# Attention with decay and an MLP on one core: one early load of q and k, one later product of v, one PSUM pair taken from another pool

## The chip, the core and the metric

The kernel runs on one core of one Trainium2 chip. The metric is the device time of one execution in microseconds (us). The core's engines that matter here are TensorE (PE; its weight loads are listed as PEld), VectorE (DVE), ScalarE (ACT), GpSimd (POOL) and SyncE (SP), which here only issues transfers. Each engine works through its own instructions in order; they meet through semaphores. Transfers between device memory (DRAM) and SBUF, the on-chip memory, run on 16 DMA engines and are issued from SP's or POOL's queue. Matrix products are written to PSUM, which is cut into banks; this kernel mostly takes banks in pairs.

## The reference

Eight batches, eight heads, 576 positions, head dimension 64. In each head: causal attention whose scores carry a decay taken from the running sum of log f. The heads are then put side by side (512 columns) and go through an MLP of width 2048 with a tanh gelu.

```python
scores = scale * np.matmul(q, k.transpose(0, 1, 3, 2))
log_f = np.log(np.clip(f, 0.0001, 1.0))
cum = np.cumsum(log_f, axis=-1)
scores = np.where(causal, -1000000000.0, scores + cum[:, :, :, None] - cum[:, :, None, :])
attn = softmax(scores)
x = np.matmul(attn, v)            # then heads side by side: (4608, 512)
h = x @ w_in
out = gelu_tanh(h) @ w_out        # (4608, 512), float32
```

## The kernel before

Four heads of a batch are a **quad**; a batch has two, so there are 16 quads (0 to 15), and batch b holds quads 2b and 2b + 1. Buffers of a quad come in twos and are taken by the quad's number modulo 2: `k_c` and `q_c` (as loaded), `kT` and `qT` (transposed), `pt` (the exps of the scores), `vw` (v times a weight per position). `v_nat` and `xT` are taken by the batch's number modulo 2.

**Decay.** The factor exp(cum) of the query cancels against the denominator, so only exp(-cum) of the key is needed. It is worked out once in the startup (`wT`, and `w_bf` in bfloat16) and multiplied into v: `make_vw` (L137) does so for one quad with two products, 128 by 1280 and 64 by 256 elements.

**Attention of a quad i.** `load_qk(i)` (L97) issues two transfers on POOL's queue, k and then q. `transpose_qk(i)` (L128) transposes both on VectorE. `score_round(i, r)` (L155) is one of three rounds: 16 or 24 score products into two pairs of PSUM banks from the pool "s", which holds two pairs, and then two exps on ScalarE that move them into `pt` (L190). `mask(i, r)` (L196) sets the part of a strip beyond the diagonal to zero on POOL; round 0 has two such instructions, round 1 one, round 2 two. `denominators(i)` (L251) multiplies `pt` with the weights into the pair "po" (this pool holds one pair) and makes reciprocals on VectorE (a transpose `den` that reads "po", a reciprocal, a transpose `rb`). The product goes through the strips in order, and its last two parts need the two masks of round 2. `attn_out(i, y)` (L254) makes one half of the output in "po", and `normalise` (L248) multiplies it on VectorE with the reciprocals into `xT`.

**MLP of a batch.** `mlp_in(b, fts)` (L276) makes tiles of the 2048 features, eight products each, in a pair from "s" (`ps_h`), with a gelu on ScalarE behind each (L272). `mlp_out` (L287) makes tiles of 128 output rows, 16 steps of products each (`pso`, a pool of two banks); after the sixteenth VectorE copies the tile to `o_st` and SP stores it. `mlp_out` is a generator: `pull(fill, n, 32)` runs n of its steps, each as four products of 32 rows, to fill TensorE's time between pieces of attention.

**Steps.** `step(i, j, fill, fills)` (L401) interleaves the scores of quad i with the output of quad j in three rounds. In each: the scores of (i, r), then `denominators(j)` in round 0 or `attn_out(j, r - 1)` in rounds 1 and 2, then masks, then some steps of the fill. Around the change the order is: startup (quads 0 and 1 and the first two feature tiles of batch 0), `transpose_qk(2)`, the other 14 feature tiles of batch 0, three steps of the fill, `step(2, None)`, `step(3, 2)`, `step(4, 3)`, and then the MLP of batch 1. In the startup, q and k of quads 2 and 3 and half of v of batch 1 are issued on POOL's queue behind the weights of the MLP; the other half of v of batch 1 is issued on SP's queue behind q of quad 3 (L365). The order of instructions on each engine is written out by hand, as the program text has it (`tc.manual_schedule`).

Lines that the change and the prediction speak of: L105 loads of v, L99 loads of k and q, L123 loads of w_out, L130 transposes, L140 vw, L162 scores, L190 exps, L202 masks, L218 products of attention, L240 to L244 reciprocals, L249 normalise, L263 and L272 feature tiles and gelus, L295 to L301 output tiles, copies and stores.

Of the kernel before, what the change touches and what calls it, by code (L numbers as in the profile page):

```python
# [16 lines left out]
def kernel(  # L17
# [79 lines left out]
    def load_qk(i):  # L97
        b, h0 = i // QPB, 4 * (i % QPB)
        return [nc.gpsimd.dma_start(  # L99
            out=dst[i % 2].rearrange("p a d -> p (a d)"),  # L100
            in_=src[b, h0:h0 + 4].rearrange("h (p a) d -> (h p) (a d)", p=32))
            for src, dst in ((k, k_c), (q, q_c))]

    def load_v(b, eng=nc.sync, heads=slice(0, H)):
        return [eng.dma_start(  # L105
            out=v_nat[b % 2][r:, t, heads, :],
            in_=v[b, heads, s0:s0 + 128 - r, :].rearrange("h p d -> p h d"),
        ) for t, r, s0 in [(t, 0, 128 * t) for t in range(TAIL)] + [(TAIL, 128 - LAST, S - LAST)]]
# [19 lines left out]
    def transpose_qk(i):  # L128
        for src, dst in ((k_c, kT), (q_c, qT)):
            nc.vector.transpose(  # L130
                out=dst[i % 2].rearrange("p s c -> p (s c)").bitcast(FP32)
                    .rearrange("p (t a) -> p a t", a=S // 32),
                in_=src[i % 2].rearrange("p a d -> p (a d)").bitcast(FP32)
                    .rearrange("p (a d) -> p a d", d=D // 2),
            )

    def make_vw(i, eng=nc.gpsimd):  # L137
        h0 = 4 * (i % QPB)
        for p, n, slot in ((128, NT, 0), (64, 1, HEAD)):
            eng.tensor_mul(  # L140
                vw[i % 2][:p, slot:slot + n], v_nat[(i // QPB) % 2][:p, 0:n, h0:h0 + 4, :],
                wT[:p, i, 0:n, :].unsqueeze(3).to_broadcast([p, n, 4, D]))

    def bank_pair(tag, name):
        return pools[tag].tile([128, 2, 512], FP32, name=name, tag=tag)
# [9 lines left out]
    def score_round(i, r, tags=("s", "s"), masked=False):  # L155
        off, parts = rounds[r]
        n = sum(x[2] for x in parts)
        tiles = [bank_pair(x, "ps_s") for x in tags]
        kk, qq, p = kT[i % 2], qT[i % 2], pt[i % 2]
        def block(c, m0, m, k0, q0, nq, c0, fresh):  # L160
            for h in range(4):
                nc.tensor.matmul(  # L162
                    tiles[h // 2][m0:m0 + m, h % 2, c0:c0 + nq],
                    kk[32 * h:32 * h + 32, k0:k0 + m, c],
                    qq[32 * h:32 * h + 32, q0:q0 + nq, c],
                    start=(c == 0 and fresh), stop=(c == 1),
                    skip_group_check=True,
                )

        if r == 0:  # L170
            for c in range(2):
                block(c, 0, 64, 0, 0, 512, 0, True)
                block(c, 64, 64, 64, 64, 448, 64, True)
                block(c, 64, 64, S - LAST, S - LAST, LAST, 0, False)
        else:
            c0 = 0
            for (t, q0, nq) in parts:
                for c in range(2):
                    block(c, 0, 128, 128 * t, q0, nq, c0, c0 == 0)
                c0 += nq  # L180
        if masked:
            for g in range(2):
                c0 = 0
                for (t, q0, nq) in parts:
                    for x in range(2 if q0 == 128 * t else 0):
                        nc.tensor.matmul(tiles[g][:, x, c0:c0 + 128], ident, lows[t > 0],
                                         start=False, stop=True, skip_group_check=True)
                    c0 += nq
        for g in range(2):
            nc.scalar.activation(p[:, 2 * g:2 * g + 2, off:off + n],  # L190
                                 tiles[g][:, :, 0:n], AF.Exp, scale=scale)
# [4 lines left out]
    def mask(i, r):  # L196
        p = pt[i % 2]
        for (t, q0, nq) in rounds[r][1]:
            if q0 == 128 * t:
                o = strip_off[t]  # L200
                for p0, p1, pattern in (diag if t else diag_first):
                    nc.gpsimd.affine_select(  # L202
                        out=p[p0:p1, :, o:o + 128], in_=p[p0:p1, :, o:o + 128],
                        compare_op=ALU.is_ge, fill=0.0, base=0, pattern=[[0, 4]] + pattern,
                        channel_multiplier=-1)
# [45 lines left out]
    def denominators(i):  # L251
        reciprocals(i, product(i, den_groups(i), bank_pair("po", "po")))

    def attn_out(i, y, tag="po"):  # L254
        normalise(i, y, product(i, out_groups(i, y), bank_pair(tag, "po")))

    def mlp_mm(b, ft, ph, dts):
        hS = S // 2
        n = 256 * (ft // 2) % (D_FF // 2)
        w = w_in_sb[2 * ft // N_FT][:, :, n + ft % 2:n + 256:2]  # L260
        for dt in dts:
            for j in range(2):
                nc.tensor.matmul(  # L263
                    ph[:, j, 0:hS],
                    w[:, dt],
                    xT[b % 2][:, dt, hS * j:hS * (j + 1)],
                    start=(dt == 0), stop=(dt == N_DT - 1),
                )

    def gelu(b, ft, ph):  # L270
        hS, o = S // 2, S * (b % 2)
        nc.scalar.activation(  # L272
            gT[:, ft, o:o + S].rearrange("p (j n) -> p j n", j=2),
            ph[:, :, 0:hS], AF.Gelu_apprx_tanh)

    def mlp_in(b, fts):  # L276
        tiles = [bank_pair("s", "ps_h") for _ in fts]
        for dts in (range(N_DT - 1), range(N_DT - 1, N_DT)):
            for ft, ph in zip(fts, tiles):
                mlp_mm(b, ft, ph, dts)  # L280
        for ft, ph in zip(fts, tiles):
            gelu(b, ft, ph)
# [21 lines left out]
    def out_tiles(b):  # L304
        n0 = 9 * (b // 2)

        return range(n0, n0 + 4) if b % 2 == 0 else range(n0 + 4, n0 + 9)
# [93 lines left out]
    def step(i, j, fill, fills):  # L401
        for r in range(3):
            if i is not None:
                score_round(i, r)
            if j is not None:
                if r == 0:
                    denominators(j)
                else:
                    attn_out(j, r - 1, "s" if i is None and r == 1 else "po")
            if (i, r) in ((2, 0), (3, 1)):  # L410
                transpose_qk(i + 1)
            if i is not None and r > 0:
                mask(i, r - 1)
            if i is not None and r == (2 if i == 2 else 0):
                make_vw(i, nc.vector if i < 4 else nc.gpsimd)
            pull(fill, fills[r], 32)
            if i is not None and r == 2:
                mask(i, 2)
                if i < 5:
                    load_qk(i + 2)  # L420
                if i == 2:
                    load_v(2)

    def prepare(*quads):

        for i in quads:
            if i < NQ:
                transpose_qk(i)
                if i + 2 < NQ:
                    load_qk(i + 2)  # L430

    with tc.manual_schedule():
        with tc.tile_pool(name="psX", bufs=1, space=bass.MemoryType.PSUM) as pools["x"]:
            startup()
        pools["m"] = ctx.enter_context(
            tc.tile_pool(name="psM", bufs=2, space=bass.MemoryType.PSUM))
        fill = none
        for b in range(B):

            if b == 0:  # L440
                transpose_qk(2)
            else:
                mlp_in(b, (0, 1))
                for x in fill:
                    pass
                prepare(2 * b + 3, 2 * b + 4)
                if b + 2 < B:
                    load_v(b + 2)
            for ft in range(2, N_FT):
                mlp_in(b, (ft,))  # L450
            fill = mlp_out(out_tiles(b))
            if b == 0:
                pull(fill, 3)
                step(2, None, fill, (14, 8, 8))
                step(3, 2, fill, (5, 6, 5))
                step(4, 3, fill, (4, 4, 3))
            elif b + 1 < B:
                i = 2 * b + 3
                fills = (((13, 11, 13), (12, 11, 13)) if b % 2 else ((11, 8, 10), (9, 8, 10)))
                pull(fill, 2)  # L460
                step(i, i - 1, fill, fills[0])
                step(i + 1 if i + 1 < NQ else None, i, fill, fills[1])
        for x in fill:
            pass
# [30 lines left out]
```

## Time and profile before

| | us |
|---|---|
| runs before, median of 3 | 348.53 |
| lowest, highest | 347.43, 350.45 |
| profiled execution | 348.43 |
| its span | 346.7 |
| busy in the span: PE | 334.6 (97%) |
| PEld | 198.6 (57%) |
| ACT | 198.8 (57%) |
| DVE | 126.0 (36%) |
| POOL | 114.5 (33%) |

The profile is one execution. Times in a timeline count from the span's start. A row of a timeline merges like instructions that follow one another: start, length, engine, line, operation, what it writes and reads, how many, and in brackets how long the engine had been idle before it and what ended that wait. A busy TensorE isn't TensorE at its peak, since products are pipelined and their ends are modelled. The chain of waits follows the work that ended last backwards; here each piece is given with its start and length. The row of the clock (PEclk) gives in tenths what share of TensorE's full speed was granted in each of 40 equal slices of the span.

### The profile page before, as it was taken

Reading aid. Unit: us, or ns where it says so; the run is one execution under the profiler, and the core shown is the slowest. Engines: PE = TensorE matmul, PEld = TensorE weight load, DVE = VectorE, ACT = ScalarE, POOL = GpSimd, SP = SyncE. Lnnn points to the kernel's source line nnn. Section 1 sums busy time; section 2 is a strip of 40 time slices with the busy share of each in tenths; the row PEclk is TensorE's granted clock in tenths of the full one; section 3 lists DMA queues with packets and bytes.
Section 4 is the critical chain, followed back from the end, with each engine's and each line's share of the span. In section 5 each row is a group of like instructions: output and inputs, shape, how many; then the busy total and the mean of one; then the engine's idle time right before and its main releaser. Section 6 shows DMA issues by size and latency. Waiting matters only on the chain.

```text
span 346.7 us, 11040 instructions
## 1 busy us (share of the span) xinstructions
PE 334.6 (97%) x5032; PEld 198.6 (57%) x5050; DVE 126.0 (36%) x169; ACT 198.8 (57%) x244; POOL 114.5 (33%) x157
## 2 busy tenths in 40 slices
PE   7999998899999999999999999999999999999995
PEld 2457744377445774467554674457644675557642
DVE  7592066551342504433234413325133312430021
ACT  4866676476645567566655567566754566516400
POOL 6642246634262232615143241624035400200000
PEclk9999999899999999999999999999999999999999
DMA  7799979659211590019311391118201100110021
GB/s 131 171 173 211 210 186 212 130 93 229 53 64 62 115 190 34 32 62 205 72 62 35 105 203 29 40 57 179 59 32 65 48 15 2 35 62 30 2 84 68
DMA packets 45439, 33.37 MB, mean 96 GB/s; under 512 B 34288, under 2 KB 34288, under 8 KB 45392
## 3 DMA queue, kind: packets, MB, share of 16 engines
q0 software_dynamic: 7232, 14.81, 23.9%
q1 hardware_dynamic: 38160, 17.85, 19.0%
q8 instruction: 39, 0.64, 0.8%
q14 instruction: 8, 0.07, 0.1%
HBM read 36.85 MB, written 9.44 MB: 133 GB/s over the span
## 4 chain that ended last, share of the span: by engine, by line
PE 83%; DMA 5%; issue 3%; ACT 3%; DVE 3%; POOL 2%; POOLq 0%; ACTq 0%; DVEq 0%
PE ps_h L263 36%; PE pso L295 31%; PE po L218 8%; PE ps_s L162 7%; DMA q_c<-in_q_dram 4%; ACT pt L190 3%; DMA v_nat<-in_v_dram 1%; POOL v_nat L105 1%; POOL pt L202 1%; DVE xT L249 1%; DVE vw L140 1%; DVE rb L244 0%; POOL k_c L99 0%; DVE den L240 0%; DVE qT L130 0%
## 5 line engine op out<-in xcount | busy, mean ns | idle before, releaser
L295 PE MATMUL pso<-w_out_sb,gT 128*32 128x512 bf16 (+1 forms) x1892 | 132.4, 381 | 0.7
L263 PE MATMUL ps_h<-xT,w_in_sb 128*128 128x288 bf16 x1024 | 128.5, 286 | 1.1 <-DVE xT L249 0.6
L190 ACT ACTIVATE pt<-ps_s 128x1024 bf16<-128x1024 f32 x96 | 93.0, 1021 | 52.7 <-PE ps_s L162 50.1
L272 ACT ACTIVATE gT<-ps_h 128x576 bf16<-128x576 f32 x128 | 82.5, 651 | 65.2 <-PE ps_h L263 65.2
L263 PEld LDWEIGHTS <-w_in_sb 128*128 128x128 bf16 x1024 | 99.5, 98 | 31.0 <-issue 4.9
L295 PEld LDWEIGHTS <-gT 128*32 128x32 bf16 (+1 forms) x1908 | 59.3, 97 | 53.7 <-issue 1.3
L202 POOL TENSOR_SCALAR_AFFINE_SELECT pt<-pt 128x512 bf16<-128x512 bf16 (+1 forms) x70 | 46.3, 670 | 132.5 <-ACT pt L190 131.6
L300 DVE COPY o_st<-pso 128x512 f32<-128x512 f32 x36 | 24.6, 685 | 63.4 <-PE pso L295 63.2
L240 DVE STREAM_TRANSPOSE den<-po 128x576 f32<-128x576 f32 x16 | 12.5, 782 | 81.9 <-PE po L218 81.9
L249 DVE TENSOR_TENSOR xT<-po,rb 128x576 bf16<-128x576 f32 x32 | 24.0, 756 | 45.4 <-PE po L218 45.2
L162 PE MATMUL ps_s<-qT,kT 32*64 32x64 bf16 (+6 forms) x896 | 36.5, 295 | 4.1 <-DVE qT L130 3.1
L140 POOL TENSOR_TENSOR vw<-v_nat,wT 128x1280 bf16<-128x1280 f32 (+1 forms) x24 | 34.8, 1472 | 1.9 <-DVE o_st L300 1.8
L162 PEld LDWEIGHTS <-kT 32*128 32x128 bf16 (+1 forms) x896 | 15.2, 98 | 30.0 <-issue 24.0
L218 PE MATMUL po<-pt,vw 128*32 128x64 bf16 (+4 forms) x768 | 27.5, 280 | 0.5 <-DVE xT L249 0.3
L130 DVE STREAM_TRANSPOSE kT<-k_c 128x576 f32<-128x576 f32 x16 | 20.0, 1247 | 16.8 <-DMA k_c<-in_k_dram 16.8
L218 PEld LDWEIGHTS <-vw 128*32 128x32 bf16 x768 | 13.4, 97 | 14.7 <-issue 8.2
L130 DVE STREAM_TRANSPOSE qT<-q_c 128x576 f32<-128x576 f32 x16 | 19.9, 1244 | 2.8 <-DMA q_c<-in_q_dram 2.7
L99 POOL DMA_DIRECT2D k_c<-in_k_dram x16 | 9.1, 567 | 29.6 <-DVE kT L130 26.6
L218 PE MATMUL po<-pt,w_bf 128*32 128x512 bf16 (+5 forms) x384 | 14.1, 280 | 0.0
L244 DVE STREAM_TRANSPOSE rb<-rec 128x576 f32<-128x576 f32 x16 | 12.4, 778 | 0.5
L190 ACT ACT_TABLE_LOAD x7 | 9.0, 1283 | 5.9 <-PE ps_s L162 5.9
L99 POOL DMA_DIRECT2D q_c<-in_q_dram x16 | 8.6, 537 | 7.2 <-DVE qT L130 5.2
(38 smaller groups left out, 72.7 us busy)
## 6 DMA issues: line engine op xcount, KB each, us to landing
out_dram<-o_st SPq DMA_DIRECT2D x36, 256.0 KB, 2.0
v_nat<-in_v_dram SPq DMA_DIRECT2D x24, 256.0 KB, 8.1
k_c<-in_k_dram POOLq DMA_DIRECT2D x16, 288.0 KB, 6.1
q_c<-in_q_dram POOLq DMA_DIRECT2D x16, 288.0 KB, 7.3
w_in_sb<-in_moe_w_in_dram POOLq DMA_DIRECT2D x4, 512.0 KB, 9.9
w_out_sb<-in_moe_w_out_dram POOLq DMA_DIRECT2D x4, 512.0 KB, 17.6
v_nat<-in_v_dram SPq DMA_DIRECT2D x14, 128.0 KB, 4.3
v_nat<-in_v_dram POOLq DMA_DIRECT2D x8, 128.0 KB, 7.2
```

What stands on the lines that cost most here:

```text
L99: return [nc.gpsimd.dma_start(out=dst[i % 2].rearrange("p a d -> p (a d)"), in_=src[b, h0:h0 + 4].rearrange("h (p a) d -> (h p) (a d)", p=32))
L130: nc.vector.transpose(out=dst[i % 2].rearrange("p s c -> p (s c)").bitcast(FP32) .rearrange("p (t a) -> p a t", a=S // 32), in_=src[i % 2] ...
L140: eng.tensor_mul(vw[i % 2][:p, slot:slot + n], v_nat[(i // QPB) % 2][:p, 0:n, h0:h0 + 4, :], wT[:p, i, 0:n, :].unsqueeze(3).to_broadcast([ ...
L162: nc.tensor.matmul(tiles[h // 2][m0:m0 + m, h % 2, c0:c0 + nq], kk[32 * h:32 * h + 32, k0:k0 + m, c], qq[32 * h:32 * h + 32, q0:q0 + nq, c ...
L190: nc.scalar.activation(p[:, 2 * g:2 * g + 2, off:off + n], tiles[g][:, :, 0:n], AF.Exp, scale=scale)
L202: nc.gpsimd.affine_select(out=p[p0:p1, :, o:o + 128], in_=p[p0:p1, :, o:o + 128], compare_op=ALU.is_ge, fill=0.0, base=0, pattern=[[0, 4]] ...
L218: nc.tensor.matmul(po[r0:r0 + w.shape[-1], o:o + nq], w, p[:, h, col:col + nq], start=(n < 2), stop=(n in (0, len(product_parts) - 1)), sk ...
L249: nc.vector.tensor_mul(xT[i // QPB % 2][:, 2 * (i % QPB) + y, :], po, rbs[i])
L263: nc.tensor.matmul(ph[:, j, 0:hS], w[:, dt], xT[b % 2][:, dt, hS * j:hS * (j + 1)], start=(dt == 0), stop=(dt == N_DT - 1),)
L272: nc.scalar.activation(gT[:, ft, o:o + S].rearrange("p (j n) -> p j n", j=2), ph[:, :, 0:hS], AF.Gelu_apprx_tanh)
L295: nc.tensor.matmul(ps[m:m + w, :], gT[:, ft, c + m:c + m + w], w_out_sb[:, ft, :], start=(ft == 0), stop=(ft == N_FT - 1), skip_group_chec ...
L300: nc.vector.tensor_copy(st, ps)
```

## The change

Three edits.

1. In front of the feature tiles of batch 0, `transpose_qk(2)` becomes `prepare(2)`: the same two transposes, and then `load_qk(4)`. In return, step 2 doesn't issue `load_qk(4)` at its end any more, only `load_v(2)`. On POOL's queue the two loads thus move from behind the five masks of step 2 to in front of them, right behind the loads of v of the startup. Steps 3 and 4 issue the loads of quads 5 and 6 as before.
2. `make_vw(3)` moves from the first round of step 3 to its third. On VectorE its two products now stand behind the second `normalise` of quad 2, and no more behind its reciprocals.
3. The third feature tile of batch 0 (`ft == 2`) takes its pair of banks from "po", not from "s".

The order of instructions on TensorE, ScalarE and SP stays the same; VectorE has the two products, and POOL the two loads, in another place.

```diff
-    def mlp_in(b, fts):
-        tiles = [bank_pair("s", "ps_h") for _ in fts]
+    def mlp_in(b, fts, tag="s"):
+        tiles = [bank_pair(tag, "ps_h") for _ in fts]
...
-            if i is not None and r == (2 if i == 2 else 0):
+            if i is not None and r == (2 if i < 4 else 0):
                 make_vw(i, nc.vector if i < 4 else nc.gpsimd)
             pull(fill, fills[r], 32)
             if i is not None and r == 2:
                 mask(i, 2)
-                if i < 5:
-                    load_qk(i + 2)
                 if i == 2:
                     load_v(2)
+                elif i < 5:
+                    load_qk(i + 2)
...
             if b == 0:
-                transpose_qk(2)
+                prepare(2)
...
-                mlp_in(b, (ft,))
+                mlp_in(b, (ft,), "po" if b == 0 and ft == 2 else "s")
```

`prepare` is there already and is not changed:

```python
def prepare(*quads):
    for i in quads:
        if i < NQ:
            transpose_qk(i)
            if i + 2 < NQ:
                load_qk(i + 2)
```

## The prediction

> **What bounds the kernel now.** I read the page first: the span and the clock row (40 slices of 8.67 us).
>
> ```profile
> span 346.7 us, 11040 instructions
> ...
> PEclk9999999899999999999999999999999999999999
> ```
>
> The profiled execution took 348.43 us, 1.73 us more than its span and 0.10 us under the median of the runs (348.53 us), so I work on 348.43 and change nothing outside the span. One slice, the eighth (60.7 to 69.3 us), has a lower TensorE clock. The change touches the first MLP and steps 2 to 4, all in 24 to 73 us, so I looked there. Below, (i, r) means round r of quad i. The chain of waits for 52 to 74 us says why the eighth slice is special:
>
> ```profile
> 52.54 0.52 POOL k_c L99
> 53.06 7.68 DMA q_c<-in_q_dram
> ```
>
> At the end of step 2 POOL issues the loads of k and q of quad 4; q takes 7.68 us and lands at 60.74. Then comes TensorE's own timeline:
>
> ```profile
> 27.27 13.88 PE L263 MATMUL ps_h<-xT,w_in_sb 128*128 128x288 bf16 x112 [0.49 <-ACT gT L272]
> ...
> 54.64 0.87 PE L218 MATMUL po<-pt,vw 128*32 128x64 bf16 x24
> ...
> 58.37 1.26 PE L295 MATMUL pso<-w_out_sb,gT 128*32 128x512 bf16 x20
> 62.08 0.66 PE L162 MATMUL ps_s<-qT,kT 32*64 32x512 bf16 x24 [2.45 <-DVE qT L130]
> ...
> 67.15 1.03 PE L295 MATMUL pso<-w_out_sb,gT 128*32 128x512 bf16 x16
> ```
>
> There are two holes: 0.49 us in front of the third feature tile (it waits for a gelu to free a PSUM pair) and 2.45 us in front of the scores of (4, 0), which wait for the transposed q. Busy time by stretches (length, PE, PEld, DVE, ACT, POOL, then granted clock, DMA share, GB/s) shows a second price of that hole:
>
> ```profile
> 24.50:27.91 3.41, 2.28 (x17) 1.42 (x16) 1.48 (x3) 1.19 (x2) 0.94 (x2) 1.00 1.12 210
> 41.20:52.00 10.80, 10.61 (x210) 4.64 (x213) 5.99 (x6) 7.74 (x8) 3.54 (x5) 1.00 0.80 190
> 59.86:63.27 3.41, 1.19 (x44) 0.66 (x48) 2.44 (x3) 0.36 (x1) 1.86 (x4) 1.00 1.03 178
> 63.27:66.68 3.41, 3.41 (x52) 1.10 (x44) 1.83 (x3) 1.81 (x3) 3.11 (x3) 0.50 0.98 206
> ```
>
> In the 3.41 us that hold the hole, TensorE was busy 1.19/3.41 = 35%; the next 3.41 us ran at half the clock. A stretch that was 2.28/3.41 = 67% busy (24.50) cost no clock. The Trainium skill ("TensorE: Matmul & The Clock Gate", table under "Why this matters for your kernels") asks for no idle gap over about 3 us; by that a 2.45 us gap would have been free, and the trace disagrees. The length of the slow stretch does agree with the roughly 3.4 us window that the page gives.
>
> In steps 2 to 4 TensorE looks busy, but the exps set the pace. ScalarE, two exps (one per PSUM pair) a round, from (3, 1) to (4, 2):
>
> ```profile
> 54.78 1.94 ACT L190 ACTIVATE pt<-ps_s 128x1024 bf16<-128x1024 f32 x2 [0.76 <-PE ps_s L162]
> 57.46 1.94 ACT L190 ACTIVATE pt<-ps_s 128x1024 bf16<-128x1024 f32 x2 [0.74 <-PE ps_s L162]
> 62.91 1.94 ACT L190 ACTIVATE pt<-ps_s 128x1024 bf16<-128x1024 f32 x2 [3.51 <-PE ps_s L162]
> 66.44 1.94 ACT L190 ACTIVATE pt<-ps_s 128x1024 bf16<-128x1024 f32 x2 [1.60 <-PE ps_s L162]
> 69.11 1.94 ACT L190 ACTIVATE pt<-ps_s 128x1024 bf16<-128x1024 f32 x2 [0.73 <-PE ps_s L162]
> ```
>
> New scores need the pairs that the exps free, and exps need the scores: 57.46 - 54.78 = 2.68 us a round. Two rounds are longer, 5.45 us (the hole) and 3.53 us (the slow clock). What follows 69.11 hangs on that exp and on TensorE, so I take the start of the exps of (4, 2) as the mark and move everything behind it as a block.
>
> **The change, part by part.**
>
> *Third feature tile in "po".* The pair was last read when the first half of quad 1's output was normalised, ahead of this tile. The 0.49 us go; the following tiles find a free "s" pair, since a tile takes 13.88/14 = 0.99 us. Bounds 0 and 0.49; I take 0.49, as nothing up to the exps of (3, 2) waits on a load that is that tight. That exp starts at 56.97 and ends at 58.91.
>
> *k and q of quad 4 earlier.* The same two loads are issued behind the v loads of startup and ahead of the masks of step 2 on POOL; SP's order stays. POOL and the transposes say when:
>
> ```profile
> 40.26 0.63 POOL L105 DMA_DIRECT2D v_nat<-in_v_dram  x1 [1.70 <-DMA w_out_sb<-in_moe_w_out_dram]
> 45.98 1.35 POOL L202 TENSOR_SCALAR_AFFINE_SELECT pt<-pt 64x512 bf16<-64x512 bf16 x2 [5.09 <-ACT pt L190]
> ...
> 54.10 2.60 POOL L202 TENSOR_SCALAR_AFFINE_SELECT pt<-pt 64x512 bf16<-64x512 bf16 x2 [0.49 <-ACT pt L190]
> ...
> 59.47 1.22 POOL L202 TENSOR_SCALAR_AFFINE_SELECT pt<-pt 128x512 bf16<-128x512 bf16 x2 [1.64 <-ACT pt L190]
> ```
>
> ```profile
> 43.90 1.26 DVE L130 STREAM_TRANSPOSE kT<-k_c 128x576 f32<-128x576 f32 x1 [10.19 <-DMA k_c<-in_k_dram]
> ...
> 54.72 2.25 DVE L140 TENSOR_TENSOR vw<-v_nat,wT 128x1280 bf16<-128x1280 f32 x2
> 56.89 0.74 DVE L249 TENSOR_TENSOR xT<-po,rb 128x576 bf16<-128x576 f32 x1
> 57.92 1.26 DVE L130 STREAM_TRANSPOSE kT<-k_c 128x576 f32<-128x576 f32 x1 [0.29 <-DMA k_c<-in_k_dram]
> 60.77 1.26 DVE L130 STREAM_TRANSPOSE qT<-q_c 128x576 f32<-128x576 f32 x1 [1.58 <-DMA q_c<-in_q_dram]
> 61.87 0.74 DVE L249 TENSOR_TENSOR xT<-po,rb 128x576 bf16<-128x576 f32 x1
> 62.54 0.67 DVE L300 COPY o_st<-pso 128x512 f32<-128x512 f32 x1
> 63.71 0.78 DVE L240 STREAM_TRANSPOSE den<-po 128x576 f32<-128x576 f32 x1 [0.50 <-PE po L218]
> ```
>
> A load on POOL waits for the load eight before it (the v load at 40.26 waited for a part of w_out). Counted on, k of quad 4 waits for the last part of w_out and q for k of quad 3, which was there at 43.90. With an issue of some 0.55 us (the chain has 0.52) the pair is out at 44.5, and the first mask behind them, 45.98 - 0.49 = 45.49, is not held: this costs nothing, and 0.55 us more if a wait is one load later. With the 7.68 us of before they land at 52.2. The stretch 41.20 to 52.00 has a DMA share of 0.80, so there is room. They are needed at 55.8 and 57.1 (next part), so 3.6 us of cover.
>
> *v of quad 3 in the third round.* VectorE's order becomes: normalise (2, first half), transposes of k and q, normalise (2, second half), v times w of quad 3, copy of o_st, transpose of den of quad 3. All times now with 0.49 taken off. The product of 54.64 ends at 55.02; normalise to 55.8 (0.74; it no longer stands behind the 2.25 us of vw); kT to 57.1 and qT to 58.4 (1.26 each); normalise to 59.1; vw would end at 61.35.
>
> TensorE: the fill of 58.37 starts at 57.88 and ends at 59.1, so scores of (4, 0) run as soon as the exps end at 58.91, and their exps start about 0.8 later, at 59.7 against 62.91. The hole is gone, 3.2 us by there. What is late next is the product of the denominators of quad 3, right behind those scores: its last third needs the two masks of the third round, which now run beside vw. The masks of 54.10 show what that costs: the pair took 2.60 us with vw starting at 54.72, against 1.35 us (45.98) with VectorE off vw. Only its second mask met vw, so a mask is held by an instruction of vw. The new masks start at 59.47 - 0.49 = 58.98 and would take 1.22 us; in turns with 2.25 us of vw both are done by 58.98 + 1.22 + 2.25 = 62.45 at the latest and 60.2 at the earliest; I take 61.5 for the masks and 61.9 for vw, near the row at 54.10, where one mask put 1.25 us on top. The Trainium skill ("SBUF — State Buffer", section "Who interferes with whom") says that a VectorE instruction with two SBUF inputs and a GpSimd instruction that reads SBUF block each other wholly; by that the sum would be the same.
>
> Behind vw: o_st to 62.6 (0.67), den to 63.4 (0.78), and only then is the pair "po" free for the first output product of quad 3. TensorE itself has finished the denominators at 61.7, the fill of 16 at 62.7 (1.03, full clock) and the scores of (4, 1) at 63.35 (0.66), so both come out together. Product to 64.3 (0.87), fill to 65.3 (1.03), scores of (4, 2), exps 0.73 later: 66.0. Against 69.11 that is 3.1 us, 0.49 from the feature tile and 2.6 from the rest. The hole and the slow clock would give more, but 1 us is handed back to vw and the masks.
>
> Sum: 348.43 - 3.1 = **345.3 us**. Bounds: if masks and vw disturb nothing, the exps keep 2.68 us a round, 59.7 + 5.36 = 65.06, a gain of 4.05: 344.4. If masks and vw end at 62.45, it is 0.5 us less gain than taken: 345.8.
>
> **The rivals.**
> - *No toll from vw* (344.3 to 344.9). For: the exps, not TensorE, set the pace, which gives slack. Against: the row at 54.10. Chance 0.22.
> - *The clock drops again.* TensorE stands in the denominators for some 1.3 to 1.7 us; a 3.41 us stretch with that is 50 to 60% busy, between the 67% that cost nothing and the 35% that did. One stretch at half the clock costs up to 3.41/2 = 1.7 us: up to 347.0. By the skill's 3 us rule above it would cost nothing. Chance 0.13.
> - *The hole stays*, because the loads land no earlier than now, or the early order is held up: only the 0.49 us, 347.9. Against: 8 us of earlier issue. Chance 0.05.
> - *Slower.* The other half of v of batch 1 comes from SP at the same time:
>
> ```profile
> 45.41 3.96 SPq L105 DMA_DIRECT2D v_nat<-in_v_dram  x5
> ```
>
> Two loads of 288 KB now run beside its five loads (576 KB). vw of quad 3 waits for it, and everything behind it on VectorE too (o_st, den, both normalisations). It decides from a landing after 59.1; each further us is a us, so 3.1 us later (62.2) all is lost, and at 66 us the kernel is over 1% slower (352). Against: 1.15 MB at the 190 GB/s of that stretch take 6.1 us from 45.41, 51.5. Chance 0.03.
>
> **How the numbers follow.** The forecast (344.9 to 345.9) has 0.57, so 345.3 us. For 8 in 10 I go down to the case without the toll and up to the case with the clock: 344.3 to 347.0. A change under 1% (3.5 us) is about what a measurement here can't tell from none; the limit is 348.53 - 3.49 = 345.04. Below it lie the first rival and about a quarter of the forecast: 0.22 + 0.14 = 0.36 faster. Slower by over 1%: 0.04. The rest, 0.60, is within 1%.
>
> **What would show it.** The 0.49 us wait on a gelu and the 2.45 us wait on qT gone; the transposes of quad 4 back to back behind the normalisation near 55.8, with no DMA wait; the clock row with no 8; masks of the third round of step 3 stretched beside vw near 59 to 62, with the denominators of quad 3 waiting on POOL; the exps of (4, 2) near 66.0. I am wrong if qT still waits on a load, if vw waits on v, or if the exps of (4, 1) start within 0.3 us of 62.4, which would be no toll.

## The result, and the profile after

| | before | after |
|---|---|---|
| median, us (4 runs each) | 348.67 (347.43 to 350.45) | 345.0 (344.53 to 345.38) |
| ratio, 95% interval | | 0.989 (0.9845 to 0.9936) |
| profiled execution / its span, us | 348.43 / 346.7 | 345.22 / 343.5 |

A second set of runs on another chip gave 344.88 against 348.33 us, ratio 0.9898 (0.9873 to 0.9923). The forecast was 345.3 us.

The page of the kernel after: the span, and the row of the clock, which has no 8 left.

```profile
span 343.5 us, 11040 instructions
...
PEclk9999999999999999999999999999999999999999
```

ScalarE's timeline, the exps from (3, 2) to (4, 2), read by their starts:

```profile
57.07 1.94 ACT L190 ACTIVATE pt<-ps_s 128x1024 bf16<-128x1024 f32 x2 [0.73 <-PE ps_s L162]
59.87 1.94 ACT L190 ACTIVATE pt<-ps_s 128x1024 bf16<-128x1024 f32 x2 [0.86 <-PE ps_s L162]
63.26 1.94 ACT L190 ACTIVATE pt<-ps_s 128x1024 bf16<-128x1024 f32 x2 [1.45 <-PE ps_s L162]
65.92 1.94 ACT L190 ACTIVATE pt<-ps_s 128x1024 bf16<-128x1024 f32 x2 [0.73 <-PE ps_s L162]
```

Before they were 5.45, 3.53 and 2.67 us apart; now 2.80, 3.39 and 2.66. The exps of (4, 2) start at 65.92 and not at 69.11: 3.19 us, and the span is 3.2 us shorter. So all of the gain is made by this mark, and nothing behind it gives any back: the span less the start of these exps is 277.6 us in both profiles. The second distance is still 0.7 us over the pace of 2.68. TensorE's timeline shows why:

```profile
57.64 1.25 PE L295 MATMUL pso<-w_out_sb,gT 128*32 128x512 bf16 x20
58.82 0.90 PE L162 MATMUL ps_s<-qT,kT 32*64 32x512 bf16 x24
59.65 0.65 PE L218 MATMUL po<-pt,w_bf 128*32 128x64 bf16 x16
60.70 0.31 PE L218 MATMUL po<-pt,w_bf 128*1 128x320 bf16 x4 [0.41 <-POOL pt L202]
61.47 0.25 PE L218 MATMUL po<-pt,w_bf 128*1 128x192 bf16 x4 [0.46 <-POOL pt L202]
61.55 1.03 PE L295 MATMUL pso<-w_out_sb,gT 128*32 128x512 bf16 x16
```

The scores of (4, 0) follow the fill with no hole. The product of the denominators, one piece before, now comes in three, and its last two parts (320 and 192 columns) each wait for a mask. POOL and VectorE at that place:

```profile
44.86 0.55 POOL L99 DMA_DIRECT2D k_c<-in_k_dram  x1 [2.13 <-DMA w_out_sb<-in_moe_w_out_dram]
46.53 0.54 POOL L99 DMA_DIRECT2D q_c<-in_q_dram  x1 [1.11 <-DMA k_c<-in_k_dram]
47.08 2.08 POOL L202 TENSOR_SCALAR_AFFINE_SELECT pt<-pt 64x512 bf16<-64x512 bf16 x3
...
59.08 2.35 POOL L202 TENSOR_SCALAR_AFFINE_SELECT pt<-pt 128x512 bf16<-128x512 bf16 x2 [1.64 <-ACT pt L190]
```

```profile
55.17 0.76 DVE L249 TENSOR_TENSOR xT<-po,rb 128x576 bf16<-128x576 f32 x1 [0.76 <-PE po L218]
55.84 1.25 DVE L130 STREAM_TRANSPOSE kT<-k_c 128x576 f32<-128x576 f32 x1
56.94 1.24 DVE L130 STREAM_TRANSPOSE qT<-q_c 128x576 f32<-128x576 f32 x1
58.02 0.74 DVE L249 TENSOR_TENSOR xT<-po,rb 128x576 bf16<-128x576 f32 x1
58.68 2.24 DVE L140 TENSOR_TENSOR vw<-v_nat,wT 128x1280 bf16<-128x1280 f32 x2
60.85 0.67 DVE L300 COPY o_st<-pso 128x512 f32<-128x512 f32 x1
61.78 0.78 DVE L240 STREAM_TRANSPOSE den<-po 128x576 f32<-128x576 f32 x1 [0.26 <-PE po L218]
```

The transposes of quad 4 wait for no load. The masks of the third round take 2.35 us for the pair (1.22 before), from 59.08 on, while vw runs from 58.68 to 60.92.

### The profile page after: what moved, and what is told of

The parts are those of the page before. It is cut to its first block, busy times and chain, and to the rows that moved or that the text cites. A ratio compares the mean times of both kernels' runs of the same rounds, so it can differ in the third digit from the quotient of the medians.

```text
span 343.5 us, 11040 instructions
## 1 busy us (share of the span) xinstructions
PE 333.7 (97%) x5032; PEld 198.1 (58%) x5050; DVE 125.3 (36%) x169; ACT 198.8 (58%) x244; POOL 113.7 (33%) x157
## 4 chain that ended last, share of the span: by engine, by line
PE 80%; DMA 11%; issue 2%; ACT 2%; POOL 2%; SPq 2%; DVE 1%; POOLq 0%; ACTq 0%
PE ps_h L263 32%; PE pso L295 32%; PE po L218 8%; PE ps_s L162 7%; DMA w_out_sb<-in_moe_w_out_dram 5%; DMA w_in_sb<-in_moe_w_in_dram 3%; DMA q_c<-in_q_dram 2%; ACT pt L190 2%; SPq L105 1%; POOL v_nat L105 1%; DMA v_nat<-in_v_dram 1%; POOL k_c L99 0%; DVE den L240 0%; DVE o_st L300 0%; POOL w_in_sb L119 0%
## 5 line engine op out<-in xcount | busy, mean ns | idle before, releaser
L202 POOL TENSOR_SCALAR_AFFINE_SELECT pt<-pt 128x512 bf16<-128x512 bf16 (+1 forms) x70 | 45.3, 656 | 125.4 <-ACT pt L190 124.4
L249 DVE TENSOR_TENSOR xT<-po,rb 128x576 bf16<-128x576 f32 x32 | 24.1, 757 | 44.9 <-PE po L218 44.5
```

Of the source, the lines that this page charges most:

```text
L202: nc.gpsimd.affine_select(out=p[p0:p1, :, o:o + 128], in_=p[p0:p1, :, o:o + 128], compare_op=ALU.is_ge, fill=0.0, base=0, pattern=[[0, 4]] ...
L249: nc.vector.tensor_mul(xT[i // QPB % 2][:, 2 * (i % QPB) + y, :], po, rbs[i])
```

## The experiments

For each kernel the table gives the median and the ratio to the runs of before on the same chip. The four distances are read from the profile: from the start of the startup's last pair of normalisations (24.66 in before) to the exps of (2, 0), and then from the exps of (3, 2) to those of (4, 0), (4, 1) and (4, 2).

| kernel | median, us | ratio, 95% interval | to (2, 0) | (4, 0) | (4, 1) | (4, 2) |
|---|---|---|---|---|---|---|
| before | | | 19.30 | 5.45 | 3.53 | 2.67 |
| after | 345.0 | 0.989 (0.9845 to 0.9936) | 18.66 | 2.80 | 3.39 | 2.66 |
| after, again | 344.88 | 0.9898 (0.9873 to 0.9923) | 18.66 | 2.80 | 3.38 | 2.67 |
| tile alone | 347.29 | 0.9976 (0.9954 to 0.9997) | 18.65 | 5.41 | 2.70 | 2.67 |
| loads alone | 345.12 | 0.9916 (0.9884 to 0.9948) | 19.30 | 3.30 | 2.69 | 2.67 |
| vw alone | 348.98 | 1.0024 (0.9994 to 1.0054) | 19.31 | 5.28 | 2.69 | 2.67 |
| loads and tile | 344.59 | 0.9900 (0.9869 to 0.9932) | 18.66 | 3.30 | 2.69 | 2.67 |
| loads and tile, again | 344.39 | 0.9884 (0.9860 to 0.9909) | 18.65 | 3.30 | 2.70 | 2.67 |
| after, no masks | 344.52 | 0.9888 (0.9861 to 0.9915) | 18.82 | 2.80 | 2.70 | 2.67 |
| before, hole filled | 347.59 | 1.0000 (0.9984 to 1.0016) | 19.30 | 5.59 | 2.70 | 2.67 |
| after, vw in pieces | 344.27 | 0.9892 (0.9870 to 0.9914) | 18.65 | 2.80 | 2.69 | 2.82 |
| other order | 343.88 | 0.9871 (0.9847 to 0.9895) | 18.65 | 2.79 | 2.70 | 2.67 |

Distances are read rather than times from the span's start because the startup itself varies: that normalisation started between 23.97 and 24.66 us in these profiles, as its v landed. Behind the last mark, the span has another 277.6 us, give or take 0.1, in all profiles but two: 278.0 in vw alone and 277.9 in the kernel with the masks left out. In these two the last twelve products of the fill of step 4 took 1.25 and 1.09 us in place of 0.82, and the trace names no wait for it.

### The tile alone

```diff
-    def mlp_in(b, fts):
-        tiles = [bank_pair("s", "ps_h") for _ in fts]
+    def mlp_in(b, fts, tag="s"):
+        tiles = [bank_pair(tag, "ps_h") for _ in fts]
...
-                mlp_in(b, (ft,))
+                mlp_in(b, (ft,), "po" if b == 0 and ft == 2 else "s")
```

> Only the third feature tile moves to the pair "po". Theory (two separate sums, 0.49 us from the tile and 2.6 us or more from the hole and what hangs on it): the wait of 0.49 us on a gelu goes, the hole in front of the scores of (4, 0) stays near 2.4 us with the half clock behind it, the exps of (4, 2) start near 68.6 instead of 69.11, ratio 0.9986 (0.9980 to 1.0000). Rival (the tile is hidden anyway, a later wait takes it back): exps of (4, 2) at 69.1, ratio 1.000. In the profile of the changed kernel a wait for w_out of 0.42 us stood behind it, so the rival is alive.

Measured: ratio 0.9976, just below the expected band, and the tile is worth more than its row said. TensorE's timeline of this kernel:

```profile
24.86 15.03 PE L263 MATMUL ps_h<-xT,w_in_sb 128*128 128x288 bf16 x120 [0.40 <-DVE xT L249]
...
60.77 0.67 PE L162 MATMUL ps_s<-qT,kT 32*64 32x512 bf16 x24 [2.41 <-DVE qT L130]
```

The 120 products now run in one piece, and the exps of (2, 0) come 18.65 us behind the mark in place of 19.30: 0.65 us, in each kernel of the table with this edit (18.82 in one, where the startup waited 0.96 us for w_in) and in none without it. The wait of 0.49 us was read from a row in which the end of the products in front of it is modelled; that this is the reason for the difference is not shown. The hole of 2.4 us stays, as the theory had it. But the exps of (4, 1) followed at 2.70 in this profile: the same hole, and no slow clock, so that the exps of (4, 2) started at 66.97 and not near 68.6.

### The loads alone

```diff
-                if i < 5:
-                    load_qk(i + 2)
                 if i == 2:
                     load_v(2)
+                elif i < 5:
+                    load_qk(i + 2)
...
-                transpose_qk(2)
+                prepare(2)
```

> Only the loads of quad 4 move; vw of quad 3 stays in the first round of step 3. Theory: the transposes of quad 4 come behind vw (2.25 us) and a normalisation, end near 60.1, hole 0.5 to 1 us, clock full, masks of the third round undisturbed (1.22 us a pair), the exps of (4, 2) near 66.6, ratio 0.993. Rival (vw has to move with the loads, because the second half of v now lands later): VectorE waits over 1 us for v in front of vw, the hole stays over 1.5 us and the clock may drop, exps of (4, 2) after 67.5, ratio 0.996 to 1.000.

Measured: 0.9916, a gain of some 2.9 us by itself, close to the theory's 0.993. VectorE's timeline:

```profile
54.57 2.25 DVE L140 TENSOR_TENSOR vw<-v_nat,wT 128x1280 bf16<-128x1280 f32 x2
56.74 0.74 DVE L249 TENSOR_TENSOR xT<-po,rb 128x576 bf16<-128x576 f32 x1
57.41 1.24 DVE L130 STREAM_TRANSPOSE kT<-k_c 128x576 f32<-128x576 f32 x1
58.50 1.23 DVE L130 STREAM_TRANSPOSE qT<-q_c 128x576 f32<-128x576 f32 x1
```

vw does not wait for v, so the rival falls. The transposes end 2.4 us behind the start of the exps of (3, 2) (59.73 against 57.31), 1.3 us later than in the kernel after, and TensorE waits for them:

```profile
59.78 0.66 PE L162 MATMUL ps_s<-qT,kT 32*64 32x512 bf16 x24 [0.30 <-DVE qT L130]
```

The exps of (4, 0) lose 0.6 us to the pace (3.30 against 2.68). The masks of the third round are undisturbed (1.22 us the pair) and lose nothing.

### vw alone

```diff
-            if i is not None and r == (2 if i == 2 else 0):
+            if i is not None and r == (2 if i < 4 else 0):
```

> Only vw of quad 3 moves to the third round. Theory: nothing to gain, since q of quad 4 still lands near 60.7 and sets the hole; vw then runs behind the transposes near 62.6 to 64.9, the transposes for the denominators of quad 3 come 1 to 2 us later on VectorE, exps of (4, 2) at 69.1 to 70.0, ratio 1.000 to 1.003. Rival (the earlier normalisation is worth something by itself): exps of (4, 2) before 68.9, ratio 0.999 or less.

Measured: 1.0024 with an interval that holds 1. No gain, as expected. Its exps of (4, 2) started at 67.84, which the rival claimed; but this profile had no slow clock (2.69 to (4, 1)), which is worth the 0.84 us by which before is longer there, so the single profile decides nothing and the runs do. In 9 of its 12 runs the mean clock was 0.995 or less, with a median of 350.15 us; in 13 of 23 runs of before on that chip it was too, with a median of 348.80. So the move alone may well cost something in such executions; no profile here shows one. Its stretches of 3.4 us (length, then busy time of PE, PEld, DVE, ACT and POOL, granted clock, DMA share, GB/s) show the hole with a full clock behind it:

```profile
59.40:62.80 3.40, 1.15 (x44) 0.65 (x48) 2.47 (x3) 0.33 (x1) 2.06 (x4) 1.00 0.84 174
62.80:66.20 3.40, 2.90 (x76) 1.47 (x71) 3.33 (x6) 2.64 (x4) 0.00 (x0) 1.00 1.02 208
```

TensorE is busy for 34% of the first one, as in the kernel before (35%), and the second is not slow.

### Loads and tile, vw where it was

The diffs of the first two together.

> The change without its second edit: loads early and tile in "po", vw of quad 3 where it was. Theory: 0.4 us below the run with the loads alone, exps of (4, 2) near 66.2, ratio 0.991 to 0.992, so that the move of vw is worth 0.3 us at most (its toll on the masks eats what it frees). Rival (vw must move with the loads): exps of (4, 2) after 67, ratio 0.995 or more.

> Loads and tile without the move of vw, beside the changed kernel. Theory: the exps stay 3.30, 2.69 and 2.67 us apart, so 0.2 us less in sum than in the changed kernel (8.66 against 8.85): ratio to it 0.999 to 1.000. Rival (the move of vw is worth its place): slower than the changed kernel by 0.2 us or more.

> The changed kernel once more, on one chip with the next three. Theory: the wait for w_out (0.42 us) and the one for w_in (0.68 us) of its first profile belonged to a later start of the weights in that execution and aren't there in every one; starts of the exps from (3, 2) to (4, 2) stay 2.80, 3.39 and 2.66 us apart; ratio 0.988 to 0.992. Rival (the early loads push the weights back): the waits for the weights are there again.

Measured: in the first set ratio 0.9900, just below the expected band, and 0.5 us under the run with the loads alone. In the second set 344.39 us beside 344.88 for the full change on the same chip, a ratio of 0.9986, and 8.67 against 8.85 us in the three distances. So the move of vw was not worth its place: it takes the transposes from behind vw (0.5 us at the first distance) and puts the masks beside it (0.7 us at the second). The 0.2 us of the profile lie within the spread of the runs. The repeat of the kernel after had no wait for weights in its fill; those of the first profile (0.68 us on w_in at 25.51, 0.42 us on w_out at 44.36) were over before the first of the moved loads was issued at 44.86, so the loads can't have made them, and the rival on the weights falls.

### The masks left out

```diff
-                mask(i, 2)
+                if i != 3:
+                    mask(i, 2)
```

> The changed kernel without the two masks of the third round of quad 3 (that part of the attention keeps its values beyond the diagonal). Theory (the toll is the masks held by vw, and TensorE waits for them in the denominators): both waits of 0.4 to 0.5 us on POOL go, vw takes 1.8 to 1.9 us instead of 2.24, the exps of (4, 1) follow those of (4, 0) by 2.7 us instead of 3.39, sum 8.2, 0.6 us less. Rival (the pair po, read late by VectorE behind vw, sets the pace and the masks only come out at the same time): the time stays, the wait moves to the products of (4, 1) or (4, 2) on po, sum 8.7 or more.

Measured: the distance to (4, 1) falls from 3.38 to 2.70, as the theory had it; of the three distances only the first is then over the pace, by 0.1 us. One row each from TensorE and VectorE of this kernel:

```profile
59.44 0.86 PE L218 MATMUL po<-pt,w_bf 128*32 128x64 bf16 x24
```

```profile
58.47 1.79 DVE L140 TENSOR_TENSOR vw<-v_nat,wT 128x1280 bf16<-128x1280 f32 x2
```

The denominators are one piece again, and vw takes 1.79 us in place of 2.24. The toll is the masks. That vw got shorter here leaves a doubt, since "po" came free earlier with it; the kernel with vw in pieces settles it, where "po" is later than in the kernel after and (4, 1) is at the pace even so. The time moved by only 0.36 us against the repeat, and not by the 0.7 us of the distances; in the profile 0.3 us were lost again behind the last mark, as said under the table.

### The hole filled

```diff
+                warm_up(bank_pair("s", "warm"), 10)
                 step(4, 3, fill, (4, 4, 3))
```

> The kernel before, with ten products of 512 columns on blank data (into a pair of the pool s, no part of the result) in the hole in front of the scores of (4, 0); the loads stay late. Theory (the slow clock is the second price of the hole): the hole stays for the scores, exps of (4, 0) 5.4 to 5.5 us behind those of (3, 2), but the clock stays full, those of (4, 1) follow by 2.7 us in every execution, the mean clock is 0.997 or more in all runs, and the time lies at the runs of before with a full clock, about 347.0, ratio 0.996. Rival (the clock drops for another reason, or the executions with it are slower for another reason): mean clocks of 0.993 to 0.995 are still there and the time is that of before.

TensorE's timeline; the blank products stand where the hole was:

```profile
59.48 2.33 PE L319 MATMUL warm<-blank 128*128 128x512 bf16 x9
62.14 0.67 PE L162 MATMUL ps_s<-qT,kT 32*64 32x512 bf16 x24 [0.33 <-DVE qT L130]
```

Measured: the mean clock was 0.998 or more in all 12 runs. In 51 runs of the kernel before, over three chips, it was 0.995 or less in 27 (median 348.61 us) and above in 24 (median 347.28 us). One stretch of 3.41 us at half clock lowers the mean over the span by 3.41 / 2 / 346.7 = 0.005, so 0.995 or less stands for a drop of that length (in the other profiles a drop at the very end of the span, when TensorE is done, leaves it at 0.997 or more). So the drop of the clock does come from the hole; it comes in about half of the executions, and those are 1.3 us longer in the median. The profile of before shows 0.84 us of that, at the distance to (4, 1); where the rest comes from is not shown. The expected ratio was missed: 1.000 and not 0.996. On this chip the clock dropped in only 6 of 17 runs of before, and the scores came 0.14 us later behind the blank products (5.59). Against the other 11 runs, with a median of 347.50 us, this kernel's 347.59 is what the theory says. The row of this table that the profile of before gives, 3.53 to (4, 1), is one of an execution with the drop.

### vw in pieces

```diff
-        for p, n, slot in ((128, NT, 0), (64, 1, HEAD)):
+        whole = ((128, 0, NT, 0), (64, 0, 1, HEAD))
+        pieces = tuple((128, t, 1, t) for t in range(NT)) + ((64, 0, 1, HEAD),)
+        for p, t, n, slot in (pieces if i == 3 else whole):
             eng.tensor_mul(
-                vw[i % 2][:p, slot:slot + n], v_nat[(i // QPB) % 2][:p, 0:n, h0:h0 + 4, :],
-                wT[:p, i, 0:n, :].unsqueeze(3).to_broadcast([p, n, 4, D]))
+                vw[i % 2][:p, slot:slot + n], v_nat[(i // QPB) % 2][:p, t:t + n, h0:h0 + 4, :],
+                wT[:p, i, t:t + n, :].unsqueeze(3).to_broadcast([p, n, 4, D]))
```

> The changed kernel with vw of quad 3 cut into six instructions (one per 128 positions and the one of 64) in place of two. Theory (a mask waits for the whole VectorE instruction that runs): the first mask of the pair now waits one piece, 0.3 to 0.4 us, and the second about as long, the pair takes 1.7 to 2.0 us instead of 2.35 and the first wait of TensorE on POOL (0.41) goes or shrinks; vw gets 0.2 to 0.4 us longer and pushes po; exps (4, 0) to (4, 2) 5.7 to 6.0 us apart in place of 6.05. Rival (both engines only share speed, whatever the size of the instruction): the pair still takes 2.3 us or more.

POOL and then TensorE of this kernel (its lines stand two further down):

```profile
58.77 1.61 POOL L204 TENSOR_SCALAR_AFFINE_SELECT pt<-pt 128x512 bf16<-128x512 bf16 x2 [1.64 <-ACT pt L192]
```

```profile
60.43 0.25 PE L220 MATMUL po<-pt,w_bf 128*1 128x192 bf16 x4 [0.30 <-POOL pt L204]
...
62.66 0.86 PE L220 MATMUL po<-pt,vw 128*32 128x64 bf16 x24 [0.48 <-DVE den L242]
```

Measured: the pair of masks takes 1.61 us in place of 2.35, with the same work on both engines. So a mask waits for the instruction of vw that is running, and the size of that instruction is the wait; the rival, shared speed, falls. The rows of the kernel after say the same one by one: the first, larger product of vw took 1.47 us there, as long as in the kernel without the masks, while the mask beside it took 1.57 us instead of 0.63. The Trainium skill ("SBUF — State Buffer", section "Who interferes with whom") says that a VectorE instruction with two SBUF inputs contends with a GpSimd instruction that reads SBUF, and calls this an exclusive lock; the trace agrees: 2.35 us for the pair beside two instructions, 1.61 beside six. vw gets longer (2.94 us from 58.37) and now "po" is late by 0.48 us, which was not the limit before. Between them 0.5 us of the distances go (8.31 against 8.85). Both gains are larger than expected: the pair was to take 1.7 to 2.0 us, and the exps of (4, 2) were to start 5.7 us or more behind those of (4, 0), where it is 5.51. One of the five executions took 349.56 us at a mean clock of 0.994; no profile shows where, and the table's ratio leaves it out.

### Another order on VectorE

```diff
-    def transpose_qk(i):
-        for src, dst in ((k_c, kT), (q_c, qT)):
+    def transpose_qk(i, which=slice(0, 2)):
+        for src, dst in ((k_c, kT), (q_c, qT))[which]:
...
-            if (i, r) in ((2, 0), (3, 1)):
-                transpose_qk(i + 1)
+            if (i, r) == (2, 0):
+                transpose_qk(3)
+            if (i, r) == (3, 0):
+                transpose_qk(4, slice(0, 1))
+            if (i, r) == (3, 1):
+                transpose_qk(4, slice(1, 2))
...
-            if i is not None and r == (2 if i < 4 else 0):
+            if i is not None and r == {2: 2, 3: 1}.get(i, 0):
```

The slice picks k or q.

> The changed kernel with another order on VectorE in step 3: transpose of k of quad 4 in the first round, that of q and then vw of quad 3 in the second, normalisation of the second half behind it. Theory (what is left over the pace of 2.68 us a round is in the changed kernel the toll of vw on masks, 0.7 us, and without the move the late transposes, 0.6 us; neither is needed): q is ready before the exps of (3, 2) end, vw is nearly over when the masks of the third round start, the exps are 2.7 to 2.85 us apart three times, 8.1 to 8.3 in sum, 0.5 to 0.7 us less than the changed kernel, ratio 0.987 to 0.990. Rival (VectorE is short of time in these rounds, whatever the order): the sum stays at 8.7 or more, with a wait on the late normalisation or on po.

VectorE's and POOL's timelines of this kernel:

```profile
53.66 1.22 DVE L130 STREAM_TRANSPOSE kT<-k_c 128x576 f32<-128x576 f32 x1
54.72 0.75 DVE L249 TENSOR_TENSOR xT<-po,rb 128x576 bf16<-128x576 f32 x1
55.38 1.24 DVE L130 STREAM_TRANSPOSE qT<-q_c 128x576 f32<-128x576 f32 x1
56.45 1.98 DVE L140 TENSOR_TENSOR vw<-v_nat,wT 128x1280 bf16<-128x1280 f32 x2
58.36 0.74 DVE L249 TENSOR_TENSOR xT<-po,rb 128x576 bf16<-128x576 f32 x1
```

```profile
58.41 1.22 POOL L202 TENSOR_SCALAR_AFFINE_SELECT pt<-pt 128x512 bf16<-128x512 bf16 x2 [1.65 <-ACT pt L190]
```

Measured: 343.88 us, 1.0 us under the kernel after on the same chip, 0.7 of it in the distances (8.16 against 8.85). vw ends at 58.43 as the masks begin at 58.41, and q is ready at 56.62, before the exps of (3, 2) end at 58.34. The kernel after left VectorE idle for 0.76 us in front of the normalisation at 55.17; a transpose (1.22 us) goes there and puts that normalisation off by only 0.2 us (1.00 us behind the exps of (3, 1), and 0.77 in the kernel after). This kernel has the lowest median and the lowest ratio of the table.

## Why the prediction was right

- **Where the time is made.** The mark was forecast at 66.0 and came at 65.92. The span followed it within 0.1 us, so what lies behind it moved as a block. That it came within 0.08 us is partly luck: the exps of (4, 0) came 0.17 us later than the 59.7 of the forecast, and the two distances behind them were 0.25 us shorter (6.05 against 6.3).
- **The tile.** Right in kind, too small: 0.49 taken, 0.65 measured. In the first profile 0.28 us of it went to a wait for w_out, so that the exps of (3, 2) came at 57.07 and not at 56.97.
- **The loads.** Forecast to be issued by 44.5 and to land at 52.2. The weights ran about 2 us later in that execution: q was issued at 46.53 and took 5.6 us, to 52.1. The cover held: q was needed at 56.94. The first mask of step 2 was to be undisturbed and was held back to 47.08; that cost nothing, as nobody needed it before the denominators of quad 2 at 51.50.
- **The hole.** Exps of (4, 0) forecast 2.73 us behind those of (3, 2), measured 2.80.
- **The new wait.** Masks beside vw: forecast done by 61.5, with the denominators waiting on POOL and finished at 61.7. Measured 61.43 and 61.72. The kernel without the masks shows that this wait is the whole toll.
- **vw itself and "po".** Too late by 0.8 to 1 us: vw was to end at 61.9 and "po" to be free at 63.4, both as late as TensorE; they came at 60.92 and 62.56. vw pays for one mask of the two and not for both: its second, smaller product took 0.85 us, and 0.41 without the masks. The 2.25 us that the forecast started from already held such a wait (0.88 us for the second product, in the row at 54.72), so it was put in twice. Another 0.4 us is the start of vw, 58.68 and not 59.1: the forecast added up the lengths of rows, and in the trace a row starts before the one ahead of it ends (the transposes of 55.84 and 56.94 are 1.25 us long and 1.10 apart). Behind the masks vw was not the limit, so the sum did not suffer.
- **The clock.** It did not drop in the new wait: the mean was 0.997 or more in the ten runs of the kernel after, and so it was in all 40 runs of the kernels with early loads and vw whole. With vw in pieces it was 0.994 in one run of five. The prediction took the slow clock of the one profile for a fixed part of the kernel before. It is a thing of about half the executions. That the median of before (348.67) lies with those, so that the sum against that profile carried over, is luck: against the runs of before without the drop (347.28) the gain is some 2.4 us and not 3.1.
- **The rivals.** No toll: the kernel without masks shows what it would be, and it was not so. The hole stays: did not come. The late v: vw of quad 3 never waited for it in any profile with early loads.
- **The chances.** 345.0 us is just under the limit of 345.04 that the prediction drew, on the side to which it gave 0.36; the repeat (344.88) is there too. The time itself lies in the range that had 0.57.

What the forecast did not see is that the second edit is not needed: the first and third alone are at least as fast.

## What to carry to other kernels

When a late load is moved forward, read which engine then carries the freed time: here VectorE's order decided the remaining 0.7 us, and an order that used its idle 0.76 us and kept vw off POOL's masks had it. Before a whole VectorE product is put beside POOL work that TensorE needs, look in the trace for a POOL instruction that was stretched by such a product; its extra time is the price, and smaller pieces lower it. Read a gain as distances between marks in the profile, since the startup alone moved by 0.7 us between executions, and see whether what lies behind the last mark stayed the same. Before a slow clock is put into a sum, look at the clock of several executions.

## What the runs showed of the hardware

A hole of 2.4 us in TensorE's work can cost half the clock for the next 3.41 us, and need not: the mean clock shows the drop in 27 of 51 executions of the kernel before. Where the hole falls may decide. In the profile of before the clock is halved from 63.27 to 66.69 us and falls again at the end of the span, at 346.58, which is 82 times 3.413 us later. So the clock seems to change only on a grid of 3.413 us. The hole of before lies in one step of this grid (59.86 to 63.27, TensorE busy 35%), and the next step is slow. In the profile of the tile alone the clock falls at 343.30, and the grid counted back from there (83 steps) has an edge at 59.99, inside the hole:

```profile
56.58:59.99 3.41, 1.78 (x44) 0.84 (x32) 1.55 (x2) 1.54 (x2) 1.80 (x4) 1.00 1.02 213
59.99:63.41 3.42, 2.46 (x66) 1.17 (x67) 2.97 (x6) 1.81 (x2) 2.09 (x2) 1.00 1.01 164
343.30:344.58 1.28, 0.00 (x0) 0.00 (x0) 0.00 (x0) 0.00 (x0) 0.00 (x0) 0.50 0.00 0
```

Here TensorE is busy for 52% and 72% of the two steps, and neither they nor the next are slow. The Trainium skill ("TensorE: Matmul & The Clock Gate", section "What's actually happening") describes a window of some 3.4 us that runs freely and isn't aligned to the kernel. The two profiles agree with that; they are too few to show it. In vw alone the stretch that was busy for 34% was not counted from an edge of the clock, and no drop followed, so a low share in some stretch of this length is not enough.

A row's wait need not be the whole price of a wait on TensorE: 0.49 us in the row were 0.64 to 0.65 us in the distances, in seven of the eight profiles with the edit.
